# Turning batch 0's first tiles uncentred, centring them in PSUM, and re-timing the slots behind them

## The chip, the cores and the metric

One Trainium2 chip, one NeuronCore of it. The metric is the device time of one execution in microseconds (us). A time quoted for a kernel is the median of its fast executions, with a granted TensorE clock of 0.987 to 1.0. "Span" is the length of the one profiled execution, about 2 us less than its time. Times within an execution count from the start of the span.

## The reference

Linear attention without a softmax, an RMS norm per head, then a layer norm with a two-layer network on top of it:

```python
kv  = einsum('bhsd,bhse->bhde', k, v)              # B=8, H=8, S=576, D=64
o   = einsum('bhsd,bhde->bhse', q, kv)
x   = o / sqrt(mean(o*o over D) + 1e-6) * g_norm   # -> [B, S, 512]
xn  = (x - mean(x)) / sqrt(var(x) + 1e-6) * g_ln
out = x + relu(xn @ w_ch1) @ w_ch2                 # 512 -> 2048 -> 512
```

Inputs and output are float32; the kernel computes its products in bf16.

## The kernel before

Each batch is four tiles of 128 rows, plus 64 rows that two batches share as a "rem" tile. The kernel scales by the layer norm's standard deviation at the very end, so what the first product needs of a tile is only xc = (x - mean) * g_ln, turned to put its 512 columns on the partitions: `xT_blk`. A tile's chain is: o on TensorE, square on ScalarE, sum on VectorE, root on ScalarE, then reciprocal, y, x and xc on VectorE, then the turn. In batch 0 and 1 the turn is done by TensorE through PSUM, later by a DMA transposition that SyncE issues.

All this small work is laid between the dense matmuls by hand. `mm1` and `mm2_part` call `tick()` before every 4 to 16 matmuls; `at(slot, fn)` puts work at a tick, and within a tick in the order of the fraction:

```python
def at(slot, fn):
    agenda.setdefault(int(slot), []).append((slot, fn))
def tick():
    for _, fn in sorted(agenda.pop(clock[0], []), key=lambda e: e[0]):
        fn()
    clock[0] += 1
def plan_tile(s, make, turn_at, on_pe):    # o, sq, red at s; y, x, xc at s+2
    ...                                    # var at s+6; the turn at turn_at
```

Three pieces: the first two are issued at slots next to each other, the third starts the loads of the batch after it:

```python
def kv_of(b):                     # 40 matmuls, then two copies on ScalarE
    kv_ps = ps_m.tile([128, HP, D], f32, tag="misc", name="kv_ps")
    ...
    nc.scalar.copy(kvp[:D, :, :D], kv_ps[:D])
    nc.scalar.copy(kvp[D:, :, D:], kv_ps[D:])

def turn_q_dma(b):                # one pass on VectorE, one transfer from SyncE
    q_p = kv_in.tile([128, JJ, H, D], bf16, tag="qp", bufs=2)
    nc.vector.tensor_copy(q_p.rearrange("p j h d -> p h j d"), q_in[b % NB])
    q_t = qt_pool.tile([128, JJ, HP, 128], bf16, tag="qt", name="qt")
    nc.sync.dma_start_transpose(q_t..., q_p...)

def load_batch(b, *after):        # waits for the elements in `after`, then loads k, v, q
    for element in after:
        nc.gpsimd.tensor_copy(gate, element)
    ...
```

`ps_m` is a PSUM pool of one buffer; the turn of a tile of batch 1 by TensorE takes the same buffer. The loads of batch b are gated on the last element of batch b - 1's turned queries, `qts[b - 1]`. The input buffers are two deep.

## Time and profile before

| | before |
|---|---|
| time, median of 3 | 290.59 us (290.45 to 290.88) |
| span of the profiled execution | 288.8 us |
| TensorE busy | 280.9 us, 97% |
| first matmul of `mm1` / first of `mm2` | 14.95 us / 32.98 us |
| queries of batch 2: VectorE's copy, transfer issued, landed | 55.45, 56.30, 61.18 us |

The timeline of VectorE, at the copies of the queries of batch 2 and of batch 3 (columns: start, duration, engine, line, operation, out<-in, and in brackets idle time before it and what ended it):

```profile
55.45 0.82 DVE L203 COPY q_p<-q_in 128x2560 bf16<-128x2560 bf16 x1
...
76.77 0.82 DVE L203 COPY q_p<-q_in 128x2560 bf16<-128x2560 bf16 x1
```

and the timeline of GpSimd where it opens the loads of batch 3:

```profile
61.23 0.18 POOL L98 COPY gate<-qt 1x1 bf16<-1x1 bf16 x1 [21.55 <-DMA qt<-q_p]
61.72 0.68 POOL L93 DMA_DIRECT2D k_in<-in_k_dram  x1 [0.31 <-issue]
```

The gate opens 0.05 us after batch 2's queries have landed: GpSimd has waited 21.55 us for them. The queries of batch 3 then land at 75.29 us and VectorE copies them at 76.77 with no wait in brackets, so 1.5 us of slack stood between the two. TensorE has no lines here; nothing in the middle of the kernel waits long enough to be named.

### The profile page before, as it was taken

The numbers are of one execution on the slowest core, as the hardware profiler recorded it, in microseconds if no ns is written. First come the engines' busy times: TensorE is split into PE (matmuls) and PEld (weight loads), VectorE is DVE, ScalarE is ACT, GpSimd is POOL, SyncE is SP. The second block draws the span as 40 slices with busy tenths as digits, with TensorE's granted clock in tenths as the row PEclk, the third lists the DMA queues.
The fourth block names the chain that finished last, engine by engine and source line by source line (L and its number), as shares of the span: only waits on it lengthen the run. The fifth ranks groups of instructions, "written<-read, shape, count | busy, mean of one in ns | idle before, by whom it ended". The sixth has DMA issues, their size and how long they took to land.

```text
span 288.8 us, 5753 instructions
## 1 busy us (share of the span) xinstructions
PE 280.9 (97%) x2295; PEld 157.9 (55%) x2295; DVE 149.8 (52%) x331; ACT 153.2 (53%) x333; POOL 41.0 (14%) x69
## 2 busy tenths in 40 slices
PE   7889999999999999999999999999999999999994
PEld 3579756995479644444444444444444444444444
DVE  5774119938897783764376935762578200220022
ACT  3477844985379733872288318921893066016400
POOL 8522510041005004100500032000000000000000
PEclk9999999999999999999999999999999999999999
DMA  7999999979788959996994189947203410230033
GB/s 214 199 206 205 198 190 195 214 112 193 138 173 101 194 108 157 202 159 120 157 217 68 39 152 219 155 84 149 56 18 64 101 36 0 48 81 19 0 73 75
DMA packets 67546, 36.76 MB, mean 127 GB/s; under 512 B 35516, under 2 KB 62524, under 8 KB 67520
## 3 DMA queue, kind: packets, MB, share of 16 engines
q0 software_dynamic: 28528, 17.76, 43.8%
q1 hardware_dynamic: 38480, 17.91, 31.2%
q10 hardware_dynamic: 512, 0.72, 0.7%
q8 instruction: 18, 0.29, 0.4%
q14 instruction: 8, 0.07, 0.1%
HBM read 36.71 MB, written 9.44 MB: 160 GB/s over the span
## 4 chain that ended last, share of the span: by engine, by line
PE 85%; DMA 5%; DVE 5%; ACT 2%; issue 1%; SPq 1%; DVEq 0%; POOLq 0%
PE p L413 41%; PE p L429 37%; PE o_ps L271 2%; DMA v_in<-in_v_dram 2%; DMA qt<-q_p 2%; PE kv_ps L246 2%; DMA xT_blk<-xc 1%; DVE ss L298 1%; ACT m L416 1%; DVE x_blk L322 1%; DVE y L303 1%; DVE o_sb L434 1%; PE p L198 1%; SPq L205 1%; ACT rms L308 0%
## 5 line engine op out<-in xcount | busy, mean ns | idle before, releaser
L413 PE MATMUL p<-xT_blk,w_sb 128*128 128x128 bf16 (+2 forms) x1024 | 131.6, 286 | 0.6 <-DMA xT_blk<-xc 0.2
L429 PE MATMUL p<-w_sb,m 128*128 128x512 bf16 (+2 forms) x608 | 129.1, 368 | 0.0
L416 ACT ACTIVATE m<-p 128x512 bf16<-128x512 f32 x144 | 85.2, 596 | 43.0 <-PE p L413 40.5
L413 PEld LDWEIGHTS <-w_sb 128*128 128x128 bf16 x1024 | 78.7, 98 | 44.9 <-issue 1.5
L429 PEld LDWEIGHTS <-m 128*128 128x128 bf16 x608 | 57.0, 98 | 62.0
L434 DVE SCALAR_TENSOR_TENSOR o_sb<-p,rstd,x_blk 128x512 f32<-128x512 f32 (+2 forms) x38 | 27.3, 720 | 52.2 <-PE p L429 41.2
L277 ACT ACTIVATE sq<-o_ps 128x512 f32<-128x512 f32 x35 | 20.9, 596 | 41.7 <-PE o_ps L271 41.7
L298 DVE TENSOR_REDUCE ss<-sq 128x8 f32<-128x512 f32 x35 | 23.7, 678 | 13.0 <-ACT sq L277 12.9
L340 ACT ACTIVATE dev<-x_blk,st_blk 128x512 f32<-128x512 f32 x36 | 25.7, 714 | 6.2 <-DVE st_blk L326 6.1
L332 DVE SCALAR_TENSOR_TENSOR xc<-x_blk,st_blk,g_ln_sb 128x512 bf16<-128x512 f32 x34 | 25.6, 752 | 1.2
L303 DVE TENSOR_TENSOR y<-o_ps,inv 128x512 f32<-128x512 f32 x33 | 22.8, 692 | 3.4 <-PE p L413 0.5
L322 DVE SCALAR_TENSOR_TENSOR x_blk<-y,g_norm_sb 128x512 f32<-128x512 f32 x33 | 22.8, 692 | 1.1
L315 DVE RECIPROCAL inv<-rms 128x8 f32<-128x8 f32 x36 | 7.2, 201 | 23.0 <-ACT rms L308 23.0
L422 DVE RECIPROCAL rstd<-rstd 128x4 f32<-128x4 f32 x9 | 1.6, 175 | 31.2 <-ACT rstd L421 31.1
L308 ACT ACTIVATE rms<-ss,eps_sb 128x8 f32<-128x8 f32 x36 | 10.7, 296 | 11.5 <-DVE ss L298 11.4
L98 POOL COPY gate<-qt 1x1 bf16<-1x1 bf16 x5 | 0.9, 177 | 106.4 <-DMA qt<-q_p 106.4
L271 PEld LDWEIGHTS <-qt 128*128 128x128 bf16 (+1 forms) x156 | 10.2, 100 | 8.1 <-issue 1.7
L271 PE MATMUL o_ps<-kv_pack,qt 128*128 128x128 bf16 (+1 forms) x156 | 13.7, 220 | 0.2
L198 PE MATMUL p<-fill_sb 128*128 128x512 bf16 x27 | 8.0, 448 | 1.2 <-DVE eps_sb L137 1.2
L340 ACT ACTIVATION_READ_ACCUMULATOR dev<-x_blk,st_blk 128x1 f32 x36 | 6.8, 189 | 0.0
L249 ACT CAST kv_pack<-kv_ps 64x256 bf16<-64x256 f32 x7 | 2.6, 366 | 7.7 <-PE kv_ps L246 7.7
L246 PEld LDWEIGHTS <-k_in 128*64 128x64 bf16 x280 | 5.0, 112 | 2.6 <-issue 2.5
(80 smaller groups left out, 110.5 us busy)
## 6 DMA issues: line engine op xcount, KB each, us to landing
out_dram<-o_sb SPq DMA_DIRECT2D x70, 128.0 KB, 2.4
w_sb<-in_moe_w_ch_dram POOLq DMA_DIRECT2D x8, 512.0 KB, 15.2
q_in<-in_q_dram POOLq DMA_DIRECT2D x7, 320.0 KB, 12.3
k_in<-in_k_dram POOLq DMA_DIRECT2D x7, 320.0 KB, 6.0
v_in<-in_v_dram POOLq DMA_DIRECT2D x7, 320.0 KB, 8.6
q_in<-in_q_dram POOLq DMA_DIRECT2D x8, 256.0 KB, 12.3
k_in<-in_k_dram POOLq DMA_DIRECT2D x7, 256.0 KB, 6.7
v_in<-in_v_dram POOLq DMA_DIRECT2D x7, 256.0 KB, 10.6
```

Source lines behind the costliest of these rows:

```text
L198: nc.tensor.matmul(p1, lhsT=fill_sb[:, :128], rhs=fill_sb, start=True, stop=True)
L271: nc.tensor.matmul(flat[rows, hp * 128:(hp + 1) * 128], lhsT=lhsT_of(hp), rhs=kvp[:, hp, :], start=True, stop=True)
L277: nc.scalar.activation(self.sq_t, self.o_ps, func=AF.Square)
L298: nc.vector.tensor_reduce(self.ss, self.sq_t, axis=AX.X, op=ALU.add)
L303: nc.vector.tensor_mul(self.y_t, self.o_ps, self.inv().to_broadcast([128, H, D]))
L322: nc.vector.scalar_tensor_tensor(x_blk[:, ts].rearrange("p (h d) -> p h d", h=H), in0=self.y_t, scalar=1.0, in1=g_norm_sb.to_broadcast([12 ...
L332: nc.vector.scalar_tensor_tensor(self.xc_t, in0=x_blk[:, self.ts], scalar=st[:, 1, self.ts:self.ts + 1], in1=g_ln_sb, op0=ALU.add, op1=ALU ...
L340: nc.scalar.activation(dev, x_blk[:, ts], func=AF.Square, bias=st[:, 1, ts:ts + 1], accum_out=st[:, 2, ts:ts + 1])
L413: nc.tensor.matmul(p1[:, i, :], lhsT=w1_sb[:, kk, de * 128:(de + 1) * 128], rhs=blk[2][:, kk, sl], start=(kk == 0), stop=(kk == nK - 1))
L416: nc.scalar.activation(m1[:, de0:de0 + per, sl], p1, func=AF.Relu)
L429: nc.tensor.matmul(p2[:, c0:c1], lhsT=m1s[b][:, de, ts * 128:(ts + 1) * 128], rhs=w2_sb[:, de, c0:c1], start=(de == 0), stop=(de == nDe - 1))
L434: nc.vector.scalar_tensor_tensor(o_sb[:, c0:c1], in0=p2[:, c0:c1], scalar=rstds[b][:, ts:ts + 1], in1=blks[b][0][:, ts, c0:c1], op0=ALU.mu ...
```

## The change

Its intent: get TensorE dense sooner, and take the small stalls at 83 and 111 us out. Tiles 0 to 2 of batch 0 are turned before they are centred: VectorE writes the uncentred product as bf16, TensorE turns it by a matmul with the identity and adds the mean (a matmul of a constant -1/512 with a diagonal of the row sums) in the same PSUM group, and the copy out of PSUM multiplies by g_ln, which for that is turned to a column by one matmul of four rows. The last half of w2 is loaded in four pieces, batch 0's second product follows them, and nearly every slot of batches 1 to 4 is moved. The core:

```diff
+        def x_b(self):            # uncentred product, bf16, with its row sum
+            nc.vector.scalar_tensor_tensor(self.xb, in0=self.og_ps, scalar=1.0, in1=self.i, ...)
+        def mean_b(self, on_act=False):   # diag = identity * row sum, on ScalarE or VectorE
+        def turn_b(self, n=2):
+            def turned(kk):
+                nc.tensor.matmul(tps[kk // 2][:, kk % 2], lhsT=flat[:, kk * 128:(kk + 1) * 128],
+                                 rhs=identity, start=True, stop=False)
+            def centred(kk):
+                nc.tensor.matmul(tps[kk // 2][:, kk % 2], lhsT=mean_sb, rhs=self.diag,
+                                 start=False, stop=True)
+            ...
+            for kk in range(n):
+                nc.scalar.activation(dst[:, kk], tps[kk // 2][:, kk % 2], func=AF.Copy,
+                                     scale=g_lnT_sb[:, kk:kk + 1])
+            if n < nK:
+                nc.vector.tensor_mul(dst[:, n:], tps[1], g_lnT_sb[:, n:]...)
...
-    for c, xc in enumerate(halves_xc(0)):
-        half_turn(0, c, xc, nc.scalar.copy)
-    t[1].red()
-    t[1].x_g()
-    xc1 = list(halves_xc(1))
+    t[0].x_b()
+    t[0].mean_b(True)
+    t[1].red()
+    nc.vector.tensor_copy(g_lnT_sb, glT)
+    t[1].root()
+    t[0].turn_b(nK)
+    t[1].x_b()
+    t[1].mean_b()
...
-    at(14.5, q_start)
-    at(19, q_turns)
-    at(22, lambda: kv_of(1))
-    for j, s, tn in ((0, 24, 30), (1, 27, 34), (2, 31, 38), (3, 35, 42)):
-        plan_tile(s, lambda j=j: main_tile(1, j), tn, True)
+    at(16.2, q_start)
+    at(20, q_turns)
+    at(22.5, lambda: kv_of(1))
+    for j, s, x_at, tn in ((0, 24, 26, 30), (1, 27, 30.1, 34), (2, 31, 33, 38), (3, 35, 37, 42)):
+        plan_tile(s, lambda j=j: main_tile(1, j), tn, True, x_at)
...
-    at(36, lambda: kv_of(2))
-    at(36.9, lambda: turn_q_dma(2))
-    for j, s, tn in ((0, 45, 51), (1, 49, 55), (2, 53, 61), (3, 57.5, 64)):
+    at(37.5, lambda: kv_of(2))
+    at(38, lambda: turn_q_dma(2))
+    for j, s, tn in ((0, 47, 53), (1, 51, 57), (2, 55, 62.5), (3, 59.5, 66)):
```

The cut parts move the loads of q and w2, the slots of batches 3 and 4 and the passes that write x to SBUF.

More of the change, by code (lines that the diff above doesn't have):

```diff
@@ L107, in load_w1, with load_w2 @@
             w1_sb[:, :, sl], moe_w_ch1[:, sl].rearrange("(ko p) n -> p ko n", p=128))
-    def load_w2(c):
-        n = nDe // 4
+    def load_w2(de0, de1):
         nc.gpsimd.dma_start(
-            w2_sb[:, c * n:(c + 1) * n, :],
-            moe_w_ch2[c * n * 128:(c + 1) * n * 128, :].rearrange("(ko p) n -> p ko n", p=128))
+            w2_sb[:, de0:de1, :],
+            moe_w_ch2[de0 * 128:de1 * 128, :].rearrange("(ko p) n -> p ko n", p=128))
     def pairs(t, hp0, hp1):
@@ L122 @@
     gate = consts.tile([1, 1], bf16)
+    mean_sb = consts.tile([128, 128], bf16)
+    gl_rows = consts.tile([nK, 128], f32)
+    four_sb = consts.tile([nK, nK], f32)
+    g_lnT_sb = consts.tile([128, nK], f32)
+    nc.vector.memset(mean_sb, -1.0 / Dm)
     nc.vector.memset(fill_sb, 0.0)
@@ L131 @@
     make_identity(nc, identity)
-    nc.gpsimd.dma_start(q_in[0][64:, :, :J], up(q, 0))
+    nc.gpsimd.dma_start(q_in[0][64:, :, :2], up(q, 0)[:, :, :2])
     load_w1(1)
     load_w1(2)
+    nc.gpsimd.dma_start(q_in[0][64:, :, 2:J], up(q, 0)[:, :, 2:])
     load_w1(3)
@@ L148 @@
                 ap=[[0, 4], list(g_norm.ap[0])]))
+    nc.sync.dma_start(gl_rows, bass.AP(tensor=moe_g_ln.tensor, offset=moe_g_ln.offset,
+                                       ap=[[128, nK], [1, 128]]))
     nc.vector.memset(kv_pack[0], 0.0)
@@ L155 @@
         nc.vector.memset(t, 0.0)
-    load_w2(0)
-    load_w2(1)
+    load_w2(0, 4)
+    load_w2(4, 8)
     for dst, src in ((q_in, q), (k_in, k), (v_in, v)):
         load(dst[1], src, 1)
-    load_w2(2)
-    load_w2(3)
+    for de in range(8, nDe, 2):
+        load_w2(de, de + 2)
     qts, held, blks, rstds, m1s, q_ps = {}, {}, {}, {}, {}, {}
@@ L284, in o_g @@
                                  rhs=kv_g[:, hp, :], start=True, stop=True)
+        def x_b(self):
+            _, st, _ = self.blk
+            self.i = self.inv().to_broadcast([128, H, D])
+            self.xb = work.tile([128, H, D], bf16, tag="xc", bufs=4, name="xb")
+            nc.vector.scalar_tensor_tensor(
+                self.xb, in0=self.og_ps, scalar=1.0, in1=self.i, op0=ALU.mult, op1=ALU.mult,
+                accum_out=st[:, 0, self.ts:self.ts + 1])
+        def mean_b(self, on_act=False):
+            self.diag = work.tile([128, 128], bf16, tag="diag", name="diag")
+            total = self.blk[1][:, 0, self.ts:self.ts + 1]
+            if on_act:
+                nc.scalar.activation(self.diag, identity, func=AF.Copy, scale=total)
+            else:
+                nc.vector.tensor_scalar_mul(self.diag, identity, total)
+        def turn_b(self, n=2):
+            ts = self.ts
+            flat = self.xb.rearrange("p h d -> p (h d)")
+            tps = [ps_out.tile([128, 2, 128], f32, tag="ops", name="tp") for _ in range(2)]
+            def turned(kk):
[4 more added lines that the diff above has]
+                                 start=False, stop=True)
+            turned(0)
+            turned(2)
+            for kk in range(0, nK, 2):
+                centred(kk)
+                turned(kk + 1)
+                centred(kk + 1)
+            dst = self.blk[2][:, :, ts * 128:(ts + 1) * 128]
+            for kk in range(n):
+                nc.scalar.activation(dst[:, kk], tps[kk // 2][:, kk % 2], func=AF.Copy,
+                                     scale=g_lnT_sb[:, kk:kk + 1])
+            if n < nK:
+                nc.vector.tensor_mul(dst[:, n:], tps[1],
+                                     g_lnT_sb[:, n:].rearrange("p (k o) -> p k o", o=1)
+                                     .to_broadcast([128, nK - n, 128]))
+            del self.xb, self.diag
         def x_g(self):
@@ L288, in x_g @@
             ts = self.ts
-            nc.vector.scalar_tensor_tensor(
-                x_blk[:, ts].rearrange("p (h d) -> p h d", h=H), in0=self.og_ps, scalar=1.0,
-                in1=self.inv().to_broadcast([128, H, D]), op0=ALU.mult, op1=ALU.mult,
-                accum_out=st[:, 0, ts:ts + 1])
+            nc.vector.tensor_mul(
+                x_blk[:, ts].rearrange("p (h d) -> p h d", h=H), self.og_ps, self.i)
             nc.vector.tensor_scalar_mul(st[:, 1, ts:ts + 1], st[:, 0, ts:ts + 1], -1.0 / Dm)
-            del self.og_ps
+            del self.og_ps, self.i
         def red(self):
@@ L369, in rem_tile, with plan_tile @@
         return Tile(mms, blks["rem"], b // 2)
-    def plan_tile(s, make, turn_at, on_pe):
+    def plan_tile(s, make, turn_at, on_pe, x_at=None):
         box = []
@@ L393, in plan_tile @@
         at(s, first)
-        at(s + 2, second)
+        at(x_at or s + 2, second)
         at(s + 6, third)
@@ L426, in mm2_part @@
         for de in range(de0, de1):
-            if de % 4 == 0:
+            if (de - de0) % 4 == 0 and (de1 - de0 > 2 or ts % 2 == 0):
                 tick()
@@ L483 @@
     del gl_row
+    nc.vector.tensor_copy(four_sb, identity[:nK, :nK])
     qts[0] = qt_pool.tile([128, JJ, HP, 128], bf16, tag="qt", name="qt")
@@ L536 @@
     t[1].o_g(ps1, "p1")
-    fill(5, dead)
+    fill(1, dead)
+    glT = ps1.tile([128, nK], f32, tag="p1", name="glT")
+    nc.tensor.matmul(glT, lhsT=gl_rows, rhs=four_sb, start=True, stop=True)
+    fill(1, dead)
     del dead
-    t[0].x_g()
-    def halves_xc(i):
-        x_blk, st, _ = t[i].blk
-        for c in range(2):
-            cs = slice(c * Dm // 2, (c + 1) * Dm // 2)
-            xc = work.tile([128, Dm // 2], bf16, tag="xch", bufs=4, name="xc")
-            nc.vector.scalar_tensor_tensor(xc, in0=x_blk[:, i, cs], scalar=st[:, 1, i:i + 1],
-                                           in1=g_ln_sb[:, cs], op0=ALU.add, op1=ALU.mult)
-            yield xc
-    def half_turn(i, c, xc, copy):
-        tp = ps_out.tile([128, 2, 128], bf16, tag="ops", name="tp")
-        for kk in range(2):
-            nc.tensor.transpose(tp[:, kk, :], xc[:, kk * 128:(kk + 1) * 128], identity)
-        copy(t[i].blk[2][:, 2 * c:2 * c + 2, i * 128:(i + 1) * 128], tp)
-    for c, xc in enumerate(halves_xc(0)):
-        half_turn(0, c, xc, nc.scalar.copy)
-    t[1].red()
-    t[1].x_g()
-    xc1 = list(halves_xc(1))
+    t[0].x_b()
+    t[0].mean_b(True)
+    t[1].red()
+    nc.vector.tensor_copy(g_lnT_sb, glT)
+    del glT
+    t[1].root()
+    t[0].turn_b(nK)
+    t[1].x_b()
+    t[1].mean_b()
     def before_1():
         turn_first(2, ps_m, "misc")
-        tp = ps2.tile([128, HP, 128], bf16, tag="p2", name="tp")
-        turn_groups(tp, 3, 0, H)
-        half_turn(1, 0, xc1[0], nc.scalar.copy)
+        t[1].turn_b()
         t[2].o()
-        half_turn(1, 1, xc1[1], nc.vector.tensor_copy)
         t[2].sq()
-        nc.scalar.copy(qts[0][:, 3], tp)
+        t[0].x_g()
         t[2].red()
         t[2].root()
-        del tp, xc1[:]
     def before_2():
         t[2].o_g(ps2, "p2")
-        t[2].x_g()
-        t[2].xc()
+        t[2].x_b()
+        t[2].mean_b()
+        t[1].x_g()
     def before_5():
@@ L588, in before_5 @@
         t[3].xc()
+        t[2].x_g()
     def next_loads():
@@ L596 @@
     at(2, before_2)
-    at(5, lambda: t[2].turn(True))
+    at(5, lambda: t[2].turn_b())
+    at(4, lambda: turn_first(3, ps_m, "misc"))
     at(5.1, before_5)
     at(9.5, next_loads)
-    at(11, lambda: t[3].turn(True))
+    at(11.9, lambda: t[3].turn(True))
     for i in range(4):
         at(16 + i, lambda i=i: t[i].var())
-    at(20, lambda: (rstd_of(0), t.clear()))
+    at(20.3, lambda: (rstd_of(0), t.clear()))
     def q_start():
@@ L627 @@
-    at(36.9, lambda: turn_q_dma(2))
-    for j, s, tn in ((0, 45, 51), (1, 49, 55), (2, 53, 61), (3, 57.5, 64)):
+    at(37.5, lambda: kv_of(2))
+    at(38, lambda: turn_q_dma(2))
+    for j, s, tn in ((0, 47, 53), (1, 51, 57), (2, 55, 62.5), (3, 59.5, 66)):
         plan_tile(s, lambda j=j: main_tile(2, j), tn, False)
-    plan_tile(62, lambda: rem_tile(1), 69, False)
+    plan_tile(64, lambda: rem_tile(1), 71, False)
     at(78, lambda: rstd_of(2))
-    for b in range(3, B):
-        s = 32 * b
-        at(47 if b == 3 else s - 60,
-           lambda b=b: load_batch(b, qts[b - 1][:1, J, HP - 1, 127:],
-                                  *([blks[2][2][:1, nK - 1, 511:]] if b == 4 else [])))
-        d = -41 if b == 3 else -45
-        at(s + d + (1 if b < 5 else 0), lambda b=b: kv_of(b))
-        at(s + d + 1.7, lambda b=b: turn_q_dma(b))
+    for b, at_load, at_kv, at_q, at_o, step in (
+            (3, 48.5, 58, 58.7, 68, 4.3), (4, 68.5, 86, 87.3, 98.5, 4.5),
+            *((b, 32 * b - 60, 32 * b - 45, 32 * b - 43.3, 32 * b - 32, 5) for b in range(5, B))):
+        at(at_load, lambda b=b: load_batch(b, qts[b - 1][:1, J, HP - 1, 127:],
+                                           *([blks[2][2][:1, nK - 1, 511:]] if b == 4 else [])))
+        at(at_kv, lambda b=b: kv_of(b))
+        at(at_q, lambda b=b: turn_q_dma(b))
@@ L641 @@
         for j in range(J):
-            o = s + d + (11 if b == 3 else 13) + 5 * j
+            o = at_o + step * j
             plan_tile(o, lambda b=b, j=j: main_tile(b, j), o + 6, False)
         if b % 2:
-            plan_tile(s - 14, lambda b=b: rem_tile(b), s - 8, False)
-        at(s + 14, lambda b=b: rstd_of(b))
+            o = 32 * b - (10.5 if b == 3 else 14)
+            plan_tile(o, lambda b=b: rem_tile(b), o + 6, False)
+        at(32 * b + 14, lambda b=b: rstd_of(b))
     at(32 * B + 14, lambda: rstd_of("rem"))
@@ L654 @@
     p2s += [ps2.tile([128, Dm], f32, tag="p2", name="p2") for _ in range(2)]
-    for de0, de1 in ((0, nDe // 2), (nDe // 2, nDe * 3 // 4)):
-        for ts in range(4):
-            mm2_part(0, ts, p2s[ts], de0, de1)
-    for ts in range(4):
-        p2 = p2s[ts]
-        p2s[ts] = None
-        mm2_part(0, ts, p2, nDe * 3 // 4, nDe)
-        finish(0, ts, p2)
-        del p2
+    for de0, de1, ts0, ts1 in ((0, 8, 0, 4), (8, 10, 0, 4), (10, 12, 0, 4), (12, 14, 0, 2),
+                               (14, 16, 0, 2), (12, 16, 2, 4)):
+        for ts in range(ts0, ts1):
+            p2 = p2s[ts]
+            mm2_part(0, ts, p2, de0, de1)
+            if de1 == nDe:
+                p2s[ts] = None
+                finish(0, ts, p2)
+            del p2
     del blks[0], m1s[0]
```

## The prediction

> **What bounds the kernel now.** I read the page first, then TensorE's waits, then the chain of waits from start to end, then the timelines of VectorE and ScalarE around each piece of that chain that is not TensorE. The page's first part:
>
> ```profile
> PE 280.9 (97%) x2295; PEld 157.9 (55%) x2295; DVE 149.8 (52%) x331; ACT 153.2 (53%) x333; POOL 41.0 (14%) x69
> ```
>
> TensorE is busy for 280.9 of 288.8 us, no other engine for more than 53%, and the granted clock is 0.998. Back to back, matmuls come every 0.216 us at 512 columns (12 in 2.59 us in the chain) and every 0.056 us at 128 columns (16 in 0.89 us). From 18.4 us on almost all time is this work, so the end is "when TensorE becomes dense, plus its work, plus the few later stalls". TensorE's waits name only these:
>
> ```profile
> PE even L225 <- DMA v_in<-in_v_dram: 1.5, 1, 1.5
> PE p L198 <- DVE eps_sb L137: 1.2, 1, 1.2
> PE tp L554 <- DVE xc L547: 0.4, 1, 0.4
> PE p L413 <- DMA xT_blk<-xc: 0.2, 1, 0.2
> ```
>
> The first two come before 8.3 us, and the change does not touch what they wait for. A matmul waiting with its weights loaded looks busy, so this view is short of the truth. I therefore took the start-to-start step of every pair of neighbouring matmuls and subtracted the streaming step. Between 13.8 and 18.3 us seven steps lose 0.19, 0.28, 0.23, 0.29, 0.56, 0.23 and 0.21 us: 1.98 us. That is batch 0's path to its first two tiles of xT, seen in the chain:
>
> ```profile
> 13.10 1.08 PE p L198 x5
> ...
> 14.20 0.30 PE tp L554 x2
> ...
> 14.52 0.37 ACT xT_blk L555
> ...
> 14.92 0.37 ACT xT_blk L555
> 15.29 0.21 ACT rms L308
> ...
> 15.84 0.71 DVE x_blk L289 x2
> ...
> 16.76 0.50 DVE xc L547
> ...
> 17.30 0.29 PE tp L554 x2
> ```
>
> Tile 1's root (15.29) stands behind tile 0's two copies on ScalarE, so tile 1's x starts at 15.84. Later steps lose 0.24 at 25.1, 0.21 at 29.2, 0.21 at 82.8 and 0.27 and 0.40 at 111.1 and 111.8 us. The last three are in the chain too:
>
> ```profile
> 78.09 4.97 DMA qt<-q_p
> ...
> 83.11 0.40 PE o_ps L271 x4
> ...
> 108.08 1.55 SPq L205
> ...
> 109.69 2.52 DMA xT_blk<-xc
> ```
>
> At 83 us four matmuls wait for batch 3's q to be turned by DMA. At 111 us batch 3's last xT was issued behind batch 4's q transfer in SyncE's queue. All losses that a reordering can reach come to 1.98 + 1.33 = 3.3 us, 1.1% of the time. A 2% gain is out of reach.
>
> **What the Trainium skill says.** "ScalarE: Activation LUTs", What ACT_TABLE_LOAD costs: an ACTIVATE with immediate scale and bias takes 186 ns + 0.833 ns per column, each [128,1] pointer operand adds about 93 ns, and neighbours overlap by about 93 ns. The trace agrees: 512 columns take 0.596 us without a pointer (the page gives 0.612) and 0.714 with one (L340; 0.706). So a 128-column copy that multiplies by g_ln from a pointer costs an estimated 0.38 us, the next starting 0.29 later. "TensorE: Matmul & The Clock Gate", Wait — 56ns, not 53.3ns?, has 55.6 and 215.7 ns for the matmul steps, as measured here. "Perfetto Trace Analysis", Transposes, asks that logical transposes use transpose and not a standard matmul. The change does the opposite; this trace has no pair to compare, so I price both at 0.056 us. "PSUM — Partial Sum Buffer", The four PSUM rules: two accumulation groups open in one bank at once spoil each other. The new order closes a group before it opens the next in its bank, so it costs no wait.
>
> **The change part by part.** Times are from the span's start.
>
> Tile 0. Before: x with its sum (12.74 to 13.43), minus mean 0.15, two halves of xc 0.88 together; the first copied half is in SBUF at 14.90, the second at 15.29. After: the same pass gives the uncentred product as bf16 at 13.43. ScalarE makes the diagonal: 0.39, to 13.87. Eight matmuls instead of four transposes; the first centring matmul starts at 13.92, the last at 14.20, and results appear 0.22 later (the length of one record). The fills (five to two, plus the four-row matmul of g_ln) are done by 13.6 and bind nothing. Tile 1's reduction now follows x at once: 13.47 to 14.15, root 14.19 to 14.49. Tile 0's four copies go behind it from 14.40: ends at 14.79, 15.08, 15.37, 15.66. Before, it was two copies of 0.37. The first group of L413 needs all four slices, then has 13 matmuls left: 15.70 + 13 x 0.056 = 16.4, against 16.2 before. Tile 0 gains nothing: 0.2 later.
>
> Tile 1. Its x starts at 14.86 instead of 15.84 and its diagonal is ready near 15.8; before, xc's second half came at 17.20. Then ScalarE binds: relu of the first group 16.6, the copy of q group 2 from 17.1 to 17.7, two xT copies to 18.25 (VectorE does the other two slices meanwhile). So tile 1's first group ends near 19.15 instead of 19.30: 0.15 gained.
>
> TensorE work added after that point: q group 3's sixteen transposes move from a stretch that waited anyway to slot 4, into dense work: 0.38 plus about 0.1 for the switch. Tile 2 has eight matmuls for four: 4 x 0.056 = 0.22. Sum 0.7. The stall at 25.1 comes from tile 3's root standing ahead of a relu on ScalarE; that order stays, but TensorE arrives later, so I count 0.1 of it as saved.
>
> Early balance: -0.15 + 0.7 - 0.1 = 0.45 us slower.
>
> Later. Batch 3's tiles move from slot 66 to 68 and their q copy goes directly behind a tile of batch 2 on VectorE: the transfer should land near 82.5 with the need at 84.6, so 0.21 saved. In SyncE's order batch 3's last xT now stands ahead of batch 4's q, and batch 4's first tile comes 2.5 slots later: 0.27 + 0.40 less about 0.1 of ordinary switching, 0.57 saved. Against it: batch 2's q copy now follows tile 3 of batch 1 on VectorE; q should land near 64.5 with TensorE there at 64.25. I count 0.15 us. Sum: 0.63 faster.
>
> Loads. The last half of w2 comes in four pieces and batch 0's second product takes them in that order. Before, its two quarters landed at 41.48 and 44.81 us and were first needed at 41.5 and 45.2: slack of 0.05 and 0.4 us. Stream and bytes stay, so pieces should land near 39.9, 41.5, 43.1 and 44.8. This gains nothing itself; it keeps an earlier TensorE from waiting. Passes of x into SBUF (L343, 0.69 each) move behind the turns, where VectorE is free. Everything from batch 5 on is unchanged.
>
> Working balance: 0.45 - 0.63 = 0.2 us faster. I choose 0.3 more, because the changed order of the q, w1 and w2 loads has a point only if TensorE reaches them sooner than before; that suggests the early part runs better than my sum. 290.59 - 0.5 = 290.1.
>
> **The rivals.**
>
> (1) The early path is a gain of 0.5 to 1 us: if a 128-column copy takes 0.2 us rather than 0.38, tile 0's group ends at 16.0 and tile 1's at 18.4. For it: xb is ready 0.7 us before the first half of xc was. Against it: the measured ScalarE durations above. It makes 289.3.
>
> (2) ScalarE becomes the bound of the first 26 us: one diagonal, eight copies of 0.38 us for four of 0.37 and one of 0.58, with relus and roots in one queue. L413 then waits for buffers freed by L416. With the late savings failing too, 291.
>
> (3) A transfer takes the place of the wait: w1's third chunk or the late quarter of q group 3 (landing an estimated 19.2 and 20.4, needed near 21), a w2 piece, or batch 2's q. Each shows as 0.2 to 0.6 us; together 290.8.
>
> (4) The late savings do not come, because the moved tiles delay each other on VectorE, which has hardly a gap between 65 and 84 us: 290.7.
>
> **Range and chances.** Known losses are 3.3 us in all, and what I add cannot exceed about 1.5. The range 289.2 to 290.9 covers rivals 1, 3 and 4 and half of 2. Both limits of 2% lie 5.8 us away: faster 0.01, same 0.98, slower 0.01.
>
> **What would show it right or wrong.** Right: L331 records of 0.37 to 0.40 us; tile 1's root before tile 0's copies, near 14.2; the first group of L413 ending at 16.2 to 16.5; no wait at batch 3's o near 84 and none for xT near 112 us; TensorE busy 0.3 to 0.7 us longer in sum. Wrong: copies near 0.2 us; dense TensorE from 17.5 or earlier; a named wait of L465 on w_sb, or of o on qt near 64 us; a time outside the range, above all below 289.2, which would mean the early path was worth more than any step here gives.

## More of the kernel before

The page's account of the chain that ended last, by engine:

```profile
PE 85%; DMA 5%; DVE 5%; ACT 2%; issue 1%; SPq 1%; DVEq 0%; POOLq 0%
```

## The result

The changed kernel is correct and slower: 294.41 us median of 4 (294.19 to 295.09), against 290.73 us (290.45 to 290.88, 4 executions) in the same rounds. The ratio is 1.0132, 95% interval 1.0112 to 1.0151. Here and below a ratio is the mean time of one kernel's fast runs over that of the other's of the same rounds, so not quite the ratio of the medians. The difference is clear of noise; at the 2% limit it still counts as "same", to which the prediction had given 0.98. The time is outside the predicted range of 289.2 to 290.9. The span of the profiled execution is 292.7 us, 3.9 us more, at a clock of 1.0.

The profile after. TensorE's row of the page and the page's account of the chain:

```profile
PE 282.6 (97%) x2306; PEld 158.9 (54%) x2306; DVE 150.4 (51%) x335; ACT 154.2 (53%) x338; POOL 43.0 (15%) x72
...
PE 77%; DMA 11%; DVE 3%; ACT 2%; POOL 2%; issue 1%; SPq 1%; DVEq 0%; POOLq 0%
```

TensorE has 1.7 us more of busy time, which the eleven extra matmuls do not fill; the share alone, again 97%, would tell nothing. The chain does: the part that is transfers has gone from 5% to 11%. Of these six points 3.7 are one load of batch 3's queries, and about one comes from the start, where the chain now runs through w1's first chunk (3.6%) and no longer through v (2.4%). The four longest of TensorE's waits (total, times, longest):

```profile
PE p L465 <- DMA xT_blk<-xc: 2.1, 2, 1.7
PE p L205 <- DVE eps_sb L142: 1.3, 1, 1.3
PE o_ps L278 <- DMA qt<-q_p: 0.9, 1, 0.9
PE tp L400 <- ACT kv_pack L257: 0.7, 1, 0.7
```

The second was there before, and the first was 0.2 us in all. All but the second lie between 56 and 93 us, past the part that the change was about. The chain, in order of time (start, duration, engine, what):

```profile
59.01 0.83 DVE q_p L210
59.86 6.70 DMA qt<-q_p
...
66.61 0.41 PE o_ps L278 x4
...
67.10 0.68 POOL k_in L93
...
70.44 10.89 DMA q_in<-in_q_dram
...
81.41 0.12 DVE q_p L210
...
89.25 3.86 DMA xT_blk<-xc
...
93.25 3.65 PE p L465 x32
```

Read downwards it is one story. The queries of batch 2 are copied at 59.01 us (before: 55.45). Their transfer is issued at 59.86 and takes 6.70 us (before: 56.30, 4.88 us). TensorE stalls for them. They also open the gate of batch 3's loads, 5.4 us later than before, so batch 3's queries land at 81.33 us instead of 75.29. Now VectorE waits for them, where before it had slack, as its timeline says:

```profile
78.31 0.75 DVE L384 SCALAR_TENSOR_TENSOR xc<-x_blk,st_blk,g_ln_sb 128x512 bf16<-128x512 f32 x1
81.41 0.83 DVE L210 COPY q_p<-q_in 128x2560 bf16<-128x2560 bf16 x1 [2.35 <-DMA q_in<-in_q_dram]
```

Tile (2,3), that is tile 3 of batch 2, stands behind that copy on VectorE, and in SyncE's queue both xT transfers of tiles (2,2) and (2,3) stand behind the transfer of batch 3's queries (SPq is that queue; its last line holds two transfers, tile (2,3)'s first):

```profile
82.27 3.05 SPq L212 DMA_TRANSPOSE qt<-q_p  x1
...
86.64 1.28 SPq L404 DMA_TRANSPOSE xT_blk<-xc  x1
...
89.25 3.89 SPq L404 DMA_TRANSPOSE xT_blk<-xc  x2
```

Tile (2,3)'s xT is issued at 89.25 us instead of 85.71, and TensorE stalls again. The smaller loss at 83 us is the wait for the xT of tiles (2,0) and (2,1), whose transfers ran beside the late loads: (2,0)'s was issued at 73.91 us and landed at 83.17, where before it went from 68.22 to 75.15.

The third wait has its own cause. ScalarE and TensorE around 57 us, from their timelines:

```profile
55.32 0.76 ACT L392 ACTIVATE dev<-x_blk,st_blk 128x512 f32<-128x512 f32 x1
...
56.26 0.35 ACT L256 CAST kv_pack<-kv_ps 64x256 bf16<-64x256 f32 x1
56.62 0.37 ACT L257 CAST kv_pack<-kv_ps 64x256 bf16<-64x256 f32 x1
```

```profile
57.03 0.38 PE L400 MATMUL tp<-identity,xc 128*128 128x128 bf16 x4 [0.67 <-ACT kv_pack L257]
```

At slot 37.5 `kv_of(2)` fills the one buffer of `ps_m` just ahead of the turn of tile (1,2) at slot 38, which needs the same buffer. The two copies that free it stand on ScalarE behind relus, `dev` and a root.

Losses of TensorE, taken as in the prediction as the start-to-start step of neighbouring matmuls less the streaming step. The kernels of the experiments are in the same table, for later; a step of about 0.10 at 83 us is an ordinary switch and is shown as none. (In the traces of e5, e6, e7 and e9 some 25 matmul records are missing; steps of exactly one missing record are left out.)

| us | before | after | e1 | e3 | e5 | e6 | e7 |
|---|---|---|---|---|---|---|---|
| first `mm2` starts | 32.98 | 33.24 | 33.35 | 32.91 | 33.39 | 33.30 | 32.74 |
| loss at 53 | - | 0.29 | 0.29 | 0.29 | 0.28 | 0.28 | 0.29 |
| loss at 56 (`ps_m`) | - | 0.83 | - | 0.83 | - | 0.84 | - |
| loss at 65 (queries of batch 2) | - | 1.09 | - | 1.04 | 1.70 | - | - |
| loss at 83 | 0.21 | 0.55 | - | 0.45 | 0.45 | - | - |
| loss at 89 to 91 (xT of tile (2,3)) | - | 1.84 | 0.54 | 2.35 | 1.44 | 0.45 | - |
| loss at 108 to 112 | 0.67 | 0.15 | 0.16 | 0.16 | 0.15 | 0.15 | 0.16 |
| queries of batch 2: issued | 56.30 | 59.86 | 56.88 | 59.53 | 60.74 | 56.83 | 56.58 |
| landed after | 4.88 | 6.70 | 4.90 | 6.65 | 5.65 | 4.89 | 4.88 |
| span | 288.8 | 292.7 | 289.1 | 292.8 | 292.0 | 289.8 | 288.3 |

From before to after: +0.26 at the first `mm2`, +0.29 + 0.83 + 1.09 + (0.55 - 0.21) + 1.84 = +4.39 in the middle, -0.52 at 111 us. The sum is 4.1 us, against 3.9 between the spans. The cause of the 0.29 at 53 us was not traced.

For differences of a few tenths the start of the span is a poor zero. The first matmul that reads v comes 8.09 to 8.41 us after it in the fourteen traces. Counted from that matmul, the first `mm2` starts after 24.64 to 24.65 us in the four traces with the old early part (before, e3, e7, e10) and after 25.09 to 25.11 us in the six with the new one unaltered (after, e1, e2, e4, e5, e6). So the early part costs TensorE 0.45 us; the +0.26 above holds 0.19 us by which v came earlier in the trace of after.

### The profile page after: what moved, and what is told of

Read it like the earlier page. It is cut to its first block, busy times and chain, and to the rows that moved or that the text cites. A ratio compares the mean times of both kernels' runs of the same rounds, so it can differ in the third digit from the quotient of the medians.

```text
span 292.7 us, 5789 instructions
## 1 busy us (share of the span) xinstructions
PE 282.6 (97%) x2306; PEld 158.9 (54%) x2306; DVE 150.4 (51%) x335; ACT 154.2 (53%) x338; POOL 43.0 (15%) x72
## 4 chain that ended last, share of the span: by engine, by line
PE 77%; DMA 11%; DVE 3%; ACT 2%; POOL 2%; issue 1%; SPq 1%; DVEq 0%; POOLq 0%
PE p L481 38%; PE p L465 36%; DMA q_in<-in_q_dram 4%; DMA w_sb<-in_moe_w_ch_dram 4%; DMA qt<-q_p 2%; PE o_ps L278 2%; DMA xT_blk<-xc 1%; PE kv_ps L253 1%; ACT m L468 1%; DVE x_blk L374 1%; DVE y L355 1%; DVE o_sb L486 1%; ACT xT_blk L402 1%; SPq L404 0%; DVE ss L350 0%
## 5 line engine op out<-in xcount | busy, mean ns | idle before, releaser
L465 PE MATMUL p<-xT_blk,w_sb 128*128 128x128 bf16 (+2 forms) x1024 | 132.2, 286 | 2.8 <-DMA xT_blk<-xc 2.1
L465 PEld LDWEIGHTS <-w_sb 128*128 128x128 bf16 x1024 | 78.5, 98 | 47.5 <-issue 2.7
L384 DVE SCALAR_TENSOR_TENSOR xc<-x_blk,st_blk,g_ln_sb 128x512 bf16<-128x512 f32 x33 | 24.8, 752 | 1.4 <-DVE st_blk L378 0.3
```

Source lines behind the costliest of these rows:

```text
L384: nc.vector.scalar_tensor_tensor(self.xc_t, in0=x_blk[:, self.ts], scalar=st[:, 1, self.ts:self.ts + 1], in1=g_ln_sb, op0=ALU.add, op1=ALU ...
L465: nc.tensor.matmul(p1[:, i, :], lhsT=w1_sb[:, kk, de * 128:(de + 1) * 128], rhs=blk[2][:, kk, sl], start=(kk == 0), stop=(kk == nK - 1))
```

## The experiments

The theory after the result: two single moves, of `kv_of(2)` from slot 36 to 37.5 and of the queries' copy of batch 2 from 36.9 to 38, made the whole loss, and the early part of the change is nearly neutral. The rivals: the early part, or the crowd of new slots, or the transfers' order, costs by itself. The expectations call the theory P and give the rivals other letters; what a letter stands for is said anew in each of them.

| kernel | time, us | before in the same rounds | ratio, 95% interval |
|---|---|---|---|
| after | 294.41 | 290.73 | 1.0132 (1.0112 to 1.0151) |
| e1_kvq2_back | 290.93 | 290.65 | 1.0008 (0.9993 to 1.0023) |
| e2_old_agenda | 293.15 | 290.65 | 1.0088 (1.0069 to 1.0107) |
| e3_new_agenda_alone | 294.48 | 290.65 | 1.0145 (1.0108 to 1.0183) |
| e4_no_gate3 | 297.81 | 290.65 | 1.0245 (1.0226 to 1.0263) |
| e5_kv2_back | 293.77 | 290.60 | 1.0133 (1.0081 to 1.0184) |
| e6_q2_only_back | 291.64 | 290.60 | 1.0046 (1.0027 to 1.0065) |
| e7_before_agenda_e1 | 289.98 | 290.60 | 0.9978 (0.9962 to 0.9995) |
| e9_tile2_old | 290.59 | 290.60 | 1.0006 (0.9991 to 1.0021) |
| e10_before_q2_late | 296.07 | 290.48 | 1.0199 (1.0179 to 1.0219) |
| e8_root1_back | 290.71 | 290.48 | 1.0004 (0.9989 to 1.0019) |
| e11_tile0_two_engines | 290.70 | 290.48 | 1.0009 (0.9992 to 1.0026) |
| e12_tile0_and_xT23_early | 290.24 | 290.48 | 0.9992 (0.9977 to 1.0007) |

Twelve kernels in three sets of four, each set on one chip with its own runs of the kernel before; all gave correct results. The ratios of e3 and e5 are pulled up by one execution each (296.64 and 296.80 us).

### Both moves undone: e1

```diff
-    at(37.5, lambda: kv_of(2))
-    at(38, lambda: turn_q_dma(2))
+    at(36, lambda: kv_of(2))
+    at(36.9, lambda: turn_q_dma(2))
```

> Theory P (place): the loss is made by two moved slots, kv of batch 2 from 36 to 37.5 and its q copy from 36.9 to 38; only these two lines are put back. P expects 290.4 us (289.9 to 290.9): the steps that lost 0.83 at 56, 1.09 at 65, 0.45 at 83 and 1.84 at 91 us go, batch 2's q lands near 61.5 to 62.5 instead of 66.56, batch 3's loads are issued near 62.5 instead of 67.1. Rival E (early part: the uncentred turn delays TensorE and ScalarE and all the rest follows): 293.5 or more. Rival S (the slots of the tiles themselves, two later for batch 2): 292 to 293, with the stall at 91 us left.

290.93 us, 0.28 over its own runs of before, where after was 3.68 over its own: two lines give back 3.4 us. That is 0.03 above P's range, and far below what E and S expected. GpSimd's gate and the loads behind it, in e1:

```profile
61.83 0.18 POOL L98 COPY gate<-qt 1x1 bf16<-1x1 bf16 x1 [18.86 <-DMA qt<-q_p]
62.31 0.68 POOL L93 DMA_DIRECT2D k_in<-in_k_dram  x1 [0.31 <-PE p L465]
```

The gate is back near where it was (61.23 before, 66.61 after). The losses at 56, 65 and 83 us are gone. 0.54 us is left at 89 us, which P had expected to go too.

### The change with the old slots: e2

```diff
-    (all slots from batch 1 on as after)
+    (all slots from batch 1 on as before)
```

> The changed kernel with every slot from batch 1 on as before; turn, loads and order of batch 0 as changed. P and S expect 290.9 us (290.6 to 291.3), which is before plus the 0.26 us by which the first L481 started later. E expects 293 or more.

293.15 us. P and S missed by 1.9 us. E's "293 or more" came true in number, but e3 below takes its cause away. The losses at 56 and 65 us are gone, as the theory of the two moves says, but TensorE loses 0.51 us at 50.3 (0.34 of it a wait for a PSUM buffer that VectorE's `o_sb` pass had not yet freed) and 1.40 us for the xT of tile (2,3), and the stall of before near 114 us is back (0.24 + 0.40). The xT transfer is issued at 86.54 us (before: 85.71) and takes 4.35 us. So the new early part and the old slots do not fit each other; which piece of the early part is at fault was not tested. With the slots that it came with the early part is nearly neutral (after is 3.68 us over its own runs of before, e3 without it 3.83; the stalls that follow take up its 0.45 us), with the old ones it costs 2.5 us, and a part that is taken out alone can tell more about the fit than about itself.

### Only the new slots: e3

```diff
 (the kernel before)
-    (all slots from batch 1 on as before)
+    (all slots from batch 1 on as after)
```

> The kernel before with only the slots from batch 1 on as changed. P and S expect nearly the whole loss: 294.0 us (293.2 to 294.8), batch 2's q landing at 65.5 or later and the stall before the second half of batch 2's first product back. E expects 291 or less.

294.48 us, with the same five losses at the same places as after (0.29, 0.83, 1.04, 0.45, 2.35). The whole loss is in the slots; nothing of it needs the new way of tiles 0 to 2.

### Batch 3's loads not gated on batch 2's queries: e4

```diff
-        at(at_load, lambda b=b: load_batch(b, qts[b - 1][:1, J, HP - 1, 127:], ...))
+        at(at_load, lambda b=b: load_batch(b, *([qts[b - 1][...]] if b > 3 else []), ...))
```

> The changed kernel; batch 3's loads no longer wait for batch 2's turned q. If the late loads are the link between the late q of batch 2 and the stalls at 83 and 91 us, these two go (0.45 and 1.84 us) while 0.29, 0.83 and 1.09 stay: 292.2 us (291.6 to 292.8), and VectorE no longer waits 2.35 us for q_in near 79 us. If the late xT comes from VectorE being full (rival V): 294 or more. If freed loads collide with batch 2's q transfer and delay it further (rival D): 293 to 294 with a longer stall at 65 us.

297.81 us, slower still: rival D's collision, 3.8 us above D's range. Without the gate the loads start sooner and share the DMA engines with the transfer of the queries, which lands 10.0 us after its issue (60.13 to 70.13):

```profile
70.17 0.40 PE L278 MATMUL o_ps<-kv_pack,qt 128*128 128x128 bf16 x4 [4.23 <-DMA qt<-q_p]
```

The Trainium skill says this in "DMA: Bandwidth & Descriptors", Issuing engines are not separate DMA queues: transfers of ScalarE, SyncE and GpSimd run on the same 16 engines and interleave. This run agrees: 10.0 us beside the loads against 6.70 without loads beside it. Batch 3's queries land at 66.94 us, and VectorE copies them at 84.21 without a wait: the wait of 2.35 us in after did come through the gate. TensorE's losses at 83 and 91 us fell to 0.17 or less, but that alone does not show that they came the same way: TensorE is some 5 us later here, and in e10 below, where the gate is in place and TensorE as late, they are gone too. For these two the evidence is the chain of after, and e6. The run also shows what the gate is for.

### One move at a time: e5 and e6

```diff
 (e5: the changed kernel with)
-    at(37.5, lambda: kv_of(2))
+    at(36, lambda: kv_of(2))
 (e6: the changed kernel with)
-    at(38, lambda: turn_q_dma(2))
+    at(36.9, lambda: turn_q_dma(2))
```

> The changed kernel with the keys and values of batch 2 (kv_of(2)) back at slot 36, while the queries' copy of batch 2 stays at slot 38. Theory P (the place of the queries' copy sets the late chain by the clock of VectorE and the transfer, so a TensorE that is earlier only waits longer for qt): the wait of 0.83 us at 56 us for the single ps_m buffer goes, but qt still lands near 66.5 and the wait there grows from 1.09 to some 1.9 us; the stalls at 83 and 91 us stay; 294.2 us (293.8 to 294.6). Rival Q (each stall is a loss of its own, they add up): 294.41 - 0.83 = 293.6 us with the wait at 65 us still near 1.1. Rival R (the place of kv_of(2) is what makes the queries late): the stalls at 65, 83 and 91 us go too and it falls to 291.

> The changed kernel with only the queries' copy of batch 2 back ahead of tile (1,3)'s chain on VectorE (slot 36.9); kv_of(2) stays at 37.5. Theory P: the 0.83 us at 56 us for ps_m stays, qt lands near 61.8, no stall at 65, none over 0.1 at 83, and 0.5 or less at 91: the kernel with both back (290.93) plus 0.83 = 291.7 us (291.3 to 292.0). Rival Q (losses add): 294.41 - 1.09 - 0.45 - 1.84 = 291.0. Rival R (kv_of(2) is the cause): nothing but the order on VectorE changes, 294.4.

e6 is a hit for theory P: 291.64 us, 0.84 left at 56 us, the queries issued at 56.83 and landed at 61.72, nothing lost at 65 or 83, 0.45 at 90. It is 1.04 us over its own runs of before, and after was 3.68 over its own: the queries' place is worth 2.6 us.

e5 came to 293.77 us, between P (293.8 to 294.6) and Q (293.6). The profile shows how: the 0.83 us for `ps_m` went, and the wait for the queries grew by 0.61 us:

```profile
PE o_ps L278 <- DMA qt<-q_p: 1.5, 1, 1.5
...
PE p L465 <- DMA xT_blk<-xc: 1.6, 2, 1.3
```

(after: 0.9 and 2.1). TensorE reached the queries earlier and they were no earlier: they landed at 66.39 us against 66.56. So P's step is seen, and with it that two stalls in a row do not add. P had not foreseen that the last stall would shrink too, from 1.84 to 1.44 us. Taken over their own runs of before, e5 gains 0.5 us on after and e6 2.6; with both undone (e1) it is 3.4.

### The queries' move alone, in the kernel before: e10

```diff
 (the kernel before)
-    at(36.9, lambda: turn_q_dma(2))
+    at(37.1, lambda: turn_q_dma(2))
```

It passes only tile (1,3)'s y, x and xc on VectorE, about 2.5 us of work.

> The kernel before, all its slots kept, with one move: the queries' copy of batch 2 (slot 36.9) goes to 37.1, behind tile (1,3)'s chain on VectorE. It is the step that the prediction waved through ('q should land near 64.5'), alone. Theory P: the copy runs near 59.4, is handed on near 60.2, lands between 65.1 (4.9 us of transfer, as before) and 66.9 (6.7 us, as after); TensorE comes to tile (2,0) at 62.45 and stalls 2.4 to 4.2 us there; the loads of batch 3 and the queries' copy of batch 3 are late by the same, and part of it comes back as a stall for xT near 90; 293.5 to 295.0 us. Rival N (the new slots of batch 2 are what costs, since they put more into the same stretch): here they are the old ones, so a stall of 1 us or less and 291.0 to 291.8.

296.07 us, 1.1 us over P's range. The stall for the queries is as P expected; what P expected to follow from it did not come. The transfer was issued at 59.93 and landed at 66.30. TensorE waited, then worked on 48 matmuls:

```profile
66.35 0.40 PE L271 MATMUL o_ps<-kv_pack,qt 128*128 128x128 bf16 x4 [4.01 <-DMA qt<-q_p]
66.58 4.32 PE L413 MATMUL p<-xT_blk,w_sb 128*128 128x128 bf16 x48
```

The same two groups in the kernel before:

```profile
62.45 0.39 PE L271 MATMUL o_ps<-kv_pack,qt 128*128 128x128 bf16 x4
62.68 2.84 PE L413 MATMUL p<-xT_blk,w_sb 128*128 128x128 bf16 x48
```

The same 48 matmuls take 4.32 us instead of 2.84. The table by stretches shows why. Each row has a stretch, its length, the busy times of five engines with their counts of instructions, then the granted clock, the DMA share and GB/s, so the clock is the third number from the end:

```profile
66.40:67.40 1.00, 1.00 (x19) 1.00 (x20) 0.00 (x0) 0.56 (x1) 0.69 (x2) 1.00 0.00 0
...
69.40:70.40 1.00, 1.00 (x13) 1.00 (x11) 0.24 (x2) 0.62 (x2) 1.00 (x3) 0.50 1.31 190
```

The steps are 0.056 us until 67.65 us, then 0.107 us (0.427 us in e4 at 512 columns) until about 71.1, then full again. At half speed those 3.4 us did the work of 1.7. The Trainium skill has this in "TensorE: Matmul & The Clock Gate", What's actually happening: an idle window of about 3.4 us halves the clock until TensorE has been busy for as long again. Both runs agree (stalls of 4.18 and 4.40 us), and the stall of 1.84 us in the changed kernel brought no drop. The sum 4.18 + 1.7 is 5.9 us against 5.4 between the spans; the loss of 0.21 at 83 us had gone, because TensorE came later. P had expected late loads and a stall for xT near 90 us as well. The loads were late, but everything that uses them was as late, and VectorE did not wait for batch 3's queries, which landed at 80.14 us:

```profile
81.48 0.82 DVE L203 COPY q_p<-q_in 128x2560 bf16<-128x2560 bf16 x1
```

So e10 prices the first waiter with the clock behind it; that a delay also costs through the gate is shown by after, e5 and e6, where TensorE itself lost less.

### The early part: e7, e9, e8, e11

e7 is the kernel before with e1's slots, so e1 without the new way of tiles 0 to 2 and without the new order of w2 and of batch 0's second product.

```diff
 (the kernel before)
-    (all slots from batch 1 on as before)
+    (all slots from batch 1 on as after, kv_of(2) at 36, turn_q_dma(2) at 36.9)
```

> The kernel before with the new slots from batch 1 on, but kv_of(2) at 36 and the queries' copy at 36.9: it is the kernel e1_kvq2_back without the new way of tiles 0 to 2, the split loads of w2 and the order of batch 0's second products. It prices the early part of the change. Theory P (the early part costs what the first second-product shows, 33.35 - 32.91 = 0.44 in these runs, and nothing later changes): 290.93 - 0.4 = 290.5 us (290.2 to 290.8), with no stall at 111 us above 0.2. Rival S (as the kernel e2_old_agenda showed, old and new parts don't fit together, so one without the other costs more): over 291.5, with a stall of o_sb or xT at 50 or 90 us.

289.98 us, 0.2 below P's range, ratio 0.9978 with an interval that excludes 1. No loss is left between 53.3 and 107 us. It is the only kernel that is faster than before beyond its interval, by 0.6 us. e3 and e7 differ in nothing but the two moves: 3.83 us over and 0.62 under their own runs of before, so with the old early part the two moves cost 4.4 us. Against e1 (another chip, so by ratios: 0.9978 against 1.0008) the early part of the change costs about 0.9 us. The traces show 0.38 of it at the first matmul of `kv_of(1)` (38.69 us in e7, 39.07 in e1), and 0.54 is the stall at 89 us that e7 does not have.

e9 is e1 with tile 2 turned the old way: `x_g`, `xc` and four transposes, four matmuls less.

```diff
 (e1 with)
-        t[2].x_b(); t[2].mean_b(); t[1].x_g()
+        t[1].x_g(); t[2].x_old(); t[2].xc()
-    at(5, lambda: t[2].turn_b())
+    at(5, lambda: t[2].turn(True))
```

> The kernel e1_kvq2_back with tile 2 of batch 0 turned the old way (centred on VectorE in bf16, four transposes, one copy on ScalarE) and tiles 0 and 1 the new way. It takes 4 matmuls of 128 columns off TensorE, 4 x 0.056 = 0.22 us. Theory P (in the early part TensorE is busy, so 4 matmuls are worth their own time): the first second-product starts at 33.1 instead of 33.35 and the time is 290.93 - 0.2 = 290.7 us. Rival T (TensorE waits there for tile 2 of batch 0 anyway, and the shorter chain of the new way is worth more than its matmuls): a new wait of L465 for xT_blk before 30 us, and the time is the same or up to 0.5 us longer.

290.59 us, ratio 1.0006 against e1's 1.0008. The ratio is raised by the profiled execution (291.39 us), which lost 0.97 us at 108 us, for the most part waiting for an `o_sb` pass; the median is at its own runs of before, where e1's is 0.28 over. The times alone do not decide. In the trace the first second-product starts 24.92 us after the first matmul that reads v, against 25.09 to 25.11 with tile 2 turned the new way: 0.18 us gained, near P's 0.22, though a step that loses 0.24 us at 25.5 came, the one that the kernel before also has at 25.1. T's wait for tile 2's xT is not there.

e8 puts the root of tile 1 back behind tile 0's copies; e11 lets VectorE write two of tile 0's four pieces.

```diff
 (e8: e1 with)                       (e11: e1 with)
-    t[1].root()                     -    t[0].turn_b(nK)
     t[0].turn_b(nK)                 +    t[0].turn_b()
+    t[1].root()
```

> The kernel e1_kvq2_back with the root of tile 1 of batch 0 back behind tile 0's four copies on ScalarE (one part of the change undone). Theory P: the first group of L465 gets its pieces 0.25 us earlier (ends near 16.1 instead of 16.34), tile 1's chain on VectorE starts 1.0 us later (its diagonal ends near 16.9 instead of 15.75) and tile 1's turn, reached by TensorE at 16.6 now, waits 0.2 to 0.5; net 0 to +0.3 us, 290.9 to 291.2. Rival U (tile 1 has slack, the root ahead only delays tile 0): -0.2 us, the first second-product at 33.1.

> The kernel e1_kvq2_back with tile 0's four pieces of xT written by ScalarE (two) and VectorE (two in one instruction), as tiles 1 and 2 already are, instead of four in a row on ScalarE. Theory P: the last piece is there near 14.85 instead of 15.4, and the waits of 0.2 us between the matmuls of the first group of L465 go; the group, which starts at 14.81 for the first chunk of w1, ends 0.4 to 0.6 us sooner; tile 1's chain on VectorE starts 0.45 later, its diagonal ends near 16.2, about when TensorE comes to it; 290.93 - 0.4 = 290.5 us (290.2 to 290.8), first second-product near 32.95. Rival V (tile 1's chain is then what TensorE waits for): the 0.45 us on VectorE comes back as a wait of the turn of tile 1; 290.8 to 291.1, first second-product 33.3.

e8: 290.71 us, ratio 1.0004, first second-product 25.10 us after the first matmul that reads v (e1: 25.11). Neither P nor U: the move of the root is worth nothing that these runs can see. e11: in the trace theory P holds, since the first second-product starts 24.72 us after the first matmul that reads v, 0.39 sooner than in e1 (at 33.03 us, for an expected 32.95), and one wait of 0.2 us is left in the first group where e1 has two. The time, 290.70 us, does not separate it from e1 (the ratios are 1.0009 and 1.0008, and one of e11's four executions was at 291.58).

### Tile (2,3)'s turn earlier: e12

```diff
 (e11 with)
-    for j, s, tn in ((0, 47, 53), (1, 51, 57), (2, 55, 62.5), (3, 59.5, 66)):
+    for j, s, tn in ((0, 47, 53), (1, 51, 57), (2, 55, 62.5), (3, 59.5, 63)):
```

> The kernel e11_tile0_two_engines with the turn of tile (2,3) at slot 63 instead of 66, so that its transfer is issued ahead of two stores. In e1_kvq2_back TensorE stalled 0.54 us at 89 us for it. Theory P: xT of tile (2,3) is issued at 83.9 instead of 85.1 and is there when TensorE comes; the 0.54 us goes and the time is 0.5 us under e11 in the same rounds. Rival W (the transfer ends at the same time whatever its place, or the stores that it passes hold up an o_sb buffer): the same as e11, with a wait of L481 for o_sb near 90 us.

290.24 us, 0.46 under e11 in the same rounds. The xT of tile (2,3) is issued at 83.50 us, ahead of two stores, and the loss at 89 us is gone. It is the best form of the change that was tried, and it is the same as the kernel before (0.9977 to 1.0007).

## Why the prediction was wrong

**The step that failed.** It is this one: "Against it: batch 2's q copy now follows tile 3 of batch 1 on VectorE; q should land near 64.5 with TensorE there at 64.25. I count 0.15 us." The move was seen and priced at one wait. e6 measured it at 2.6 us. Three things in it were off:

1. The landing. Issued at 59.86 us, with the 4.88 us of before it would have been there at 64.74, before TensorE came (65.5): even less than 0.15 us. But the transfer took 6.70 us, so TensorE lost 1.09.
2. The followers. The step asked only who waits for `qt` on TensorE. The same event opens GpSimd's gate. The 21.55 us that GpSimd had waited at that gate was in the profile of before, and showed that any delay of the queries passes on whole to the loads of batch 3. These had 1.5 us of slack at VectorE and were delayed by 5.4. That is the stall of 1.84 us at 91 us and most of 0.34 at 83. The chain of after shows this link step by step, and in e6, with the queries back in their place and all else as in after, both stalls are gone but for 0.45 us. e4, which cut the gate, removed VectorE's wait; for TensorE's stalls it proves less, as said there.
3. What was not in the text at all: `kv_of(2)` from 36 to 37.5. It puts two users of the single `ps_m` buffer next to each other, 0.83 us (e3, e6 with it; e1, e5 without). The list of slots showed it.

The prediction's third rival did name batch 2's queries as a transfer that could take the place of a wait, and its list of what would prove it wrong had a wait for them near 64 us. The size it gave, 0.2 to 0.6 us together with others, again came from looking at one waiter.

**The late savings** came as stated: 0.57 us expected at 111 us, 0.52 measured. The 0.21 at 83 us was eaten by the stall of point 2; in e1 and e6 it is there.

**The early part** was near: 0.45 us slower expected, 0.45 measured at the first second-product, counted from the first matmul that reads v. The copies of L331:

```profile
14.16 1.14 ACT L331 ACTIVATE xT_blk<-tp,g_lnT_sb 128x128 bf16<-128x128 f32 x4
```

The four records are 0.36 to 0.38 us long, as worked out, but start 0.25 to 0.27 us apart and not 0.29: neighbours overlap by 0.10 to 0.12 us here, more than the 0.09 that the prediction took from the page. The first group of L465 started at 14.72 us, after a wait of 0.43 for w1's first chunk, which landed at 14.68 us (before: 13.31). The new order of loads alone does not do this: with the same order it landed at 14.77 in e1 and at 13.20 to 13.33 us in the eight other kernels. The group ended at 16.2 us (expected 16.2 to 16.5), and w2's pieces landed at 39.99, 41.68, 43.38 and 45.06 us (39.9, 41.5, 43.1 and 44.8). The wait for w1 cost nothing in the end: e2, e4, e5 and e6 do not have it and reach the first second-product no sooner. The sum fits better than its terms: tile 2's four matmuls, counted as 0.22 - 0.1, cost 0.18 (e9); the root ahead of the copies, which the plan for tile 1 rested on, gains nothing (e8); and to split tile 0's four copies over two engines gains 0.39 (e11), which the prediction did not weigh. So the fit of the sum is in part luck. Rival 1, copies of 0.2 us, fell; rival 2, ScalarE as the bound, is seen only in these 0.39 us. TensorE's busy time rose by 1.7 us, for an expected 0.3 to 0.7.

**The added 0.3 us of trust** ("the early part runs better than my sum") had no measurement behind it, and pointed the wrong way. The range was too narrow for the same reason: its upper end held half of a named rival, and no rival followed a delay past its first waiter.

**What stays open.** Why the queries' transfer takes longer at that time. In the nine kernels that issued it between 56.3 and 57.3 us it took 4.84 to 4.90 us; in the four with the gate in place that issued it between 59.5 and 60.8 us it took 5.65 to 6.70, and landed at 66.2 to 66.6 each time. In the packet records of the traces one thing goes with it. In each of these four, and in e4, a 16 KB packet of the queue for instructions ran among the transfer's data packets or straight behind them (after: data until 64.54, that packet from 64.54 to 65.46, the transfer's last packet at 65.46; e5: data from 61.93 to 65.92, that packet from 61.88 to 63.28). In each of the nine early ones the instruction packets ended before the first data packet or started after the landing. That is a coincidence seen in fourteen traces, not a cause that was tested. What decides about the 0.3 to 0.5 us at 89 us in e1, e6, e8 and e11 is not settled either; e12 removes it, and e7 and e9 do not have it.

## What to carry to other kernels

Before moving a transfer or the work that issues it, list everybody who waits for its landing, gates of later loads first, and look up how long each of them waited before the move: an engine that waited long there has no slack at all, and passes the delay on whole. In a plan of slots, look at pairs that share a buffer of depth one whenever either of them moves. And size a stall as "what arrives late, less how late the waiter itself is": taking away an earlier stall then makes a later one longer, as in e5, and a long early stall hides later ones, as in e10. Last, measure tenths of a microsecond from an event that the stage depends on and not from the start of the span, which moved by 0.3 us here.

## What the Trainium skill lacked or had wrong

- "TensorE: Matmul & The Clock Gate" gives the idle window that halves the clock; it does not say in words that the drop can fall on work that has already started again, though one of its event lists has it 5.2 us after the last matmul. In e10 TensorE worked 1.3 us at full rate after a stall of 4.18 us, then 3.4 us at half rate, from 5.5 us after the last matmul ahead of the stall; in e4 0.6 us after a stall of 4.40, 5.0 us after the last matmul. Such a stall costs about 1.7 us more than itself.
- "DMA: Bandwidth & Descriptors" gives effective bandwidths of DMA transposition (261 GB/s on one kernel, about 350 to 400 in the contiguous case) and no time from issue to landing of one. Here a tile of 128 x 2560 bf16, 655,360 bytes, took 4.84 to 4.90 us in nine kernels, 5.65 to 6.70 us in four, and 10.0 us beside loads. 4.88 us are 134 GB/s from issue to landing; in the kernel before the data packets alone ran from 57.48 to 60.71 us, which is 203 GB/s.
- "Perfetto Trace Analysis" asks for a transpose where a matmul would do the same. For bf16 and 128 columns this study shows no price for the matmul: the four turned and four centring matmuls of tile 1 start within 0.40 us (16.54 to 16.94 us in the changed kernel), seven steps of 0.057 us, against 0.056 for a transpose.
- No page that was read says in words that a transfer which gates others is to be counted with its followers; here an issue that was 3.6 us later cost 2.6 us, in three places.
